# Keys of the second batch turned by a DMA transpose in place of TensorE transposes and ScalarE copies

## The chip, the cores and the metric

The kernel runs on one core of one Trainium2 chip. The time is the device time of one execution in microseconds (us), as the median of several executions. All runs told of here are in the fast state, with one core at work. A ratio is always the mean time of one kernel's fast runs over the mean time of the fast runs of the kernel before, of the same rounds on the same chip, so it is not quite the ratio of the medians that are quoted beside it. Intervals are 95% intervals.

## The reference

Sparse attention, then a gated feed-forward layer. There are 4 batches of 8 heads, 768 positions and 64 columns per head. Each query sees the keys less than 16 positions away, and 24 summaries of the keys (the maximum of each block of 32 keys, with the mean of the values of that block). The result, as 3072 tokens of 512 columns, goes through `x + sigmoid(x @ w_res) * ((gelu(x @ w_gate) * (x @ w_val)) @ w_out)`.

```python
k_sum = k.reshape(B, H, nb, block, D).max(axis=3)       # block maxima of the keys
v_sum = v.reshape(B, H, nb, block, D).mean(axis=3)      # block means of the values
scores_l = scale * np.matmul(q, k.transpose(0, 1, 3, 2))         # masked to |i - j| < 16
scores_s = scale * np.einsum('bhsd,bhnd->bhsn', q, k_sum) + np.log(block)
# softmax over both, times [v, v_sum], then the feed-forward layer
```

## The kernel before

The work is cut into 8 units of 384 tokens, two per batch. A unit has a gate/value stage of 12 column steps (g and vv matmuls, Gelu on ScalarE, a product on VectorE), and then an output stage, which also holds the scores and the attention of the next unit. During the two units of a batch, the keys, values and queries of the next batch are loaded and brought into place. The keys have to lie with the head's columns on the partitions, so they have to be turned. The batches from the third on do this with a DMA transpose; the second batch, which is loaded while the weights are still arriving, does it on TensorE.

```python
def load_k(b, t, i, n):            # one load of 768 KB (as bf16), 2 KB pieces of the source
    hs = slice(i * H // n, (i + 1) * H // n)
    nc.gpsimd.dma_start(out=t[:, hs]..., in_=k[b, hs].rearrange("h (p j) d -> p h (j d)", j=PJ))

def load_k_nat(b):                 # keys in order: twelve loads of 64 KB, 256-byte pieces
    k_nat = qk.tile([QT, NT, DM], BF16, tag="k_nat", name="k_nat")
    for t in range(NT):
        nc.gpsimd.dma_start(out=k_nat[:, t]..., in_=k[b, :, t * QT:(t + 1) * QT, :]...)
    return k_nat

def turn_k(b, k_nat):              # one DMA transpose of the whole batch, on SyncE's queue
    nc.sync.dma_start_transpose(out=kW[b % 2]...[:, :, 0:QT], in_=k_nat...)

def turn_pair(src, hp, pool, tag): # 16 transposes on TensorE for two heads
    ...
def k_place(b, hp, tp):
    nc.scalar.copy(kW[b % 2][:, :, hp, 0:QT]..., tp...)
    k_blocks(b, hp)                # block maxima, on VectorE: a reduce and a copy
    k_rims(b, slice(hp, hp + 1), nc.vector)   # keys of the neighbouring tiles

# ---- in the loop over units u and column steps fo (cut) ----
if half == 0 and nb == 1:          # first unit: loads of the second batch
    k_sb[nb] = k_tile()
    load_k(nb, k_sb[nb], 0, 1)
    v_loads(nb)                    # twelve loads of 64 KB
    load_q_nat(nb)                 # six loads of 128 KB
...
if half == 1 and nb < B:           # second unit of a batch
    if fo == 0:
        v_rims(nb, 0, HT)          # on SyncE's queue
        ...
    if fo == (4 if nb == 1 else 1):
        vsum_grp(nb, ps_t, "t")    # value sums: 12 matmuls over all twelve value tiles
        for i in range(4):
            vsum_bc(nb, 3 * i, 3 * i + 3, nc.gpsimd)   # copies of the value means
        turn_q(nb, 0)
        turn_q(nb, 1)
    if nb == 1:
        if fo < NP:
            k_step(nb, fo, ps_t, "t")      # turn_pair, then k_place
    elif 2 <= fo < 2 + NP:
        k_blocks(nb, fo - 2)
```

The softmax here doesn't subtract the row's maximum and nothing guards it: scores larger than these inputs give would overflow.

Of the kernel before, what the change touches and what calls it, by code (L numbers as in the profile page):

```python
# [15 lines left out]
def kernel(  # L16
# [11 lines left out]
    nc = tc.nc  # L28
# [16 lines left out]
    NP = H // 2  # L45
# [16 lines left out]
    ps_t = ctx.enter_context(tc.tile_pool(name="ps_t", bufs=1, space=bass.MemoryType.PSUM))  # L62
# [23 lines left out]
    def load_k(b, t, i, n):  # L86
        hs = slice(i * H // n, (i + 1) * H // n)
        nc.gpsimd.dma_start(out=t[:, hs].rearrange("p h j d -> p h (j d)"),
                            in_=k[b, hs].rearrange("h (p j) d -> p h (j d)", j=PJ))

    def k_tile():
        return qk.tile([PP, H, PJ, D], BF16, tag="k_sb", name="k_sb")
# [8 lines left out]
    def v_loads(b, lo=0, hi=NT):  # L101
        for t in range(lo, hi):
            nc.gpsimd.dma_start(out=vext[b % 2][0:QT, t, :, 0:D],  # L103
                                in_=v[b, :, t * QT:(t + 1) * QT, :].rearrange("h p d -> p h d"))

    def v_rims(b, lo, hi, eng=nc.sync):
        x = vext[b % 2]
        a, e = min(hi, NT - 1), max(lo, 1)
        eng.dma_start(out=x[QT:QT + WIN, lo:a], in_=x[0:WIN, lo + 1:a + 1])
        eng.dma_start(out=x[QT + WIN:BAND, e:hi], in_=x[QT - WIN:QT, e - 1:hi - 1])  # L110

    k_sb, q_sb = {}, {}

    def load_k_nat(b):
        k_nat = qk.tile([QT, NT, DM], BF16, tag="k_nat", name="k_nat")
        for t in range(NT):
            nc.gpsimd.dma_start(out=k_nat[:, t].rearrange("p (h d) -> p h d", d=D),  # L117
                                in_=k[b, :, t * QT:(t + 1) * QT, :].rearrange("h p d -> p h d"))
        return k_nat

    def load_q_nat(b):
        for c in range(NQ):
            nc.gpsimd.dma_start(out=q_nat[:, c].rearrange("p (h d) -> p h d", d=D),  # L123
                                in_=q[b, :, c * 128:(c + 1) * 128, :].rearrange("h p d -> p h d"))

    def turn_k(b, k_nat):
        nc.sync.dma_start_transpose(out=kW[b % 2].rearrange("d t g k -> d (t g) k")[:, :, 0:QT],
                                    in_=k_nat.rearrange("p t f -> p (t f)"))
# [6 lines left out]
    with tc.manual_schedule():  # L135
# [65 lines left out]
        def turn_pair(src, hp, pool, tag):  # L201
            tp = pool.tile([128, PJ, PP], BF16, tag=tag, name="tp")
            for j in range(PJ):
                for hh in range(2):
                    nc.tensor.transpose(tp[hh * 64:hh * 64 + 64, j, :], src[:, 2 * hp + hh, j, :],  # L205
                                        ident[0:PP, 0:PP])
            return tp

        def k_blocks(b, hp):
            kw = kW[b % 2][:, :, hp]  # L210
            ks = work.tile([128, NB], BF16, tag="ks", name="ks")
            nc.vector.tensor_reduce(  # L212
                out=ks.rearrange("d (t n) -> d t n", n=2),
                in_=kw[:, :, 0:QT].rearrange("d t (n w) -> d t n w", w=BLK),
                axis=mybir.AxisListType.X, op=ALU.max)
            nc.vector.tensor_copy(kw[:, :, BAND:BAND + NB], ks.unsqueeze(1).to_broadcast([128, NT, NB]))

        def k_rims(b, hps, eng):
            kw = kW[b % 2][:, :, hps]
            eng.tensor_copy(kw[:, 0:NT - 1, :, QT:QT + WIN], kw[:, 1:NT, :, 0:WIN])  # L220
            eng.tensor_copy(kw[:, 1:NT, :, QT + WIN:BAND], kw[:, 0:NT - 1, :, QT - WIN:QT])

        def k_step(b, hp, pool, tag):
            k_place(b, hp, turn_pair(k_sb[b], hp, pool, tag))

        def k_place(b, hp, tp):
            nc.scalar.copy(kW[b % 2][:, :, hp, 0:QT].rearrange("d t (p j) -> d t p j", j=PJ),
                           tp.rearrange("d j (t p) -> d t p j", t=NT))
            k_blocks(b, hp)
            k_rims(b, slice(hp, hp + 1), nc.vector)  # L230
# [367 lines left out]
        def pool_after(x):  # L598
            nc.gpsimd.tensor_copy(gate2[:], x)

        for u in range(NU):
            b, half = u // 2, u % 2
            nb = b + 1
            if half == 0 and nb == 1:
                k_sb[nb] = k_tile()
                load_k(nb, k_sb[nb], 0, 1)
                v_loads(nb)
                load_q_nat(nb)
            if u:
                gvT = upool.tile([128, FO, TU], BF16, tag="gvT", name="gvT")  # L610
            for fo in range(0 if u else 2, FO):
                if u > 1 and fo == 0:
                    fo_first(st, gvT)
                elif u and fo == FO - 2:
                    fo_last_two(st, gvT)
                elif u == 0 or fo < FO - 2:
                    fo_step(st, gvT, fo)
                if u == 0:
                    unit0_extras(fo)
                if u == 0 and fo >= 8:  # L620
                    q_step(1, fo - 8, ps_t, "t")
                if half == 0 and 1 < nb < B and fo == 0:
                    pool_after(st["xT"][0:1, KO - 1, 0:1])
                    k_nat = load_k_nat(nb)
                    v_loads(nb)
                if half == 0 and b and fo == 1:
                    v_rims(b, HT, NT)
                if half == 0 and 1 < nb < B and fo == 6:
                    turn_k(nb, k_nat)
                    k_rims(nb, slice(0, NP), nc.gpsimd)  # L630
                if half == 1 and nb < B:
                    if fo == 0:
                        v_rims(nb, 0, HT)
                        if nb > 1:
                            pool_after(st["xT"][0:1, KO - 1, 0:1])
                            load_q_nat(nb)
                    if fo == (4 if nb == 1 else 1):
                        vsum_grp(nb, ps_t, "t")
                        for i in range(4):
                            vsum_bc(nb, 3 * i, 3 * i + 3, nc.gpsimd)  # L640
                        turn_q(nb, 0)
                        turn_q(nb, 1)
                    if nb == 1:
                        if fo < NP:
                            k_step(nb, fo, ps_t, "t")
                    elif 2 <= fo < 2 + NP:
                        k_blocks(nb, fo - 2)
            if u == NU - 1:
                last_out(u, st, gvT)
            else:  # L650
                nst = new_unit()
                (mid_out if u else first_out)(u, st, gvT, nst)
                st = nst
# [30 lines left out]
```

## Time and profile before

| | before |
|---|---|
| median time | 260.93 us (260.77 to 261.4; three runs, a fourth, taken later, makes it 260.85) |
| span of the profiled execution | 260.5 us (this execution took 262.43 us, 1.5 more than the median) |
| TensorE (PE) busy | 251.3 us, 96% of the span |
| second unit, first gate matmul to the third unit's | 56.37 to 87.69 us: 31.3 us |

In all views PE is TensorE, PEld its loading of weights, DVE is VectorE, ACT ScalarE, POOL GpSimd and SP SyncE, which issues DMAs; a q behind the name marks work of the queue that the engine issues to. The granted clock is the share of TensorE's full clock that it was given. The profile's page of the kernel before has the busy time of each engine, and after it the span in 40 slices (each digit a busy share in tenths; PEclk the granted TensorE clock in tenths), and the chain of work that ended last:

```profile
PE 251.3 (96%) x2294; PEld 138.1 (53%) x2294; DVE 156.1 (60%) x344; ACT 126.3 (48%) x210; POOL 104.5 (40%) x142
...
PE   6999889999999999999999999999999999999993
...
PEclk9999999999999999999999999999999999999999
...
PE 82%; DMA 11%; POOL 3%; ACT 1%; issue 1%; DVE 1%; POOLq 0%
```

TensorE is the bound: it is 96% busy and 82% of the chain. What TensorE spends or saves in the second unit counts in full.

The timeline of the kernel before (start in us, length in us, engine, line, operation, output <- inputs, count, and in brackets the idle time before it and what ended it) shows one of the four key turns between two column steps, and the value sums:

```profile
57.02 0.81 PE L356 MATMUL vv<-xT,w_val 128*128 128x384 bf16 x4
...
57.77 0.53 PE L205 MATMUL tp<-ident,k_sb 96*64 96x96 bf16 x16
...
58.23 0.82 PE L356 MATMUL g<-xT,w_gate 128*128 128x384 bf16 x4
58.34 0.80 ACT L227 COPY kW<-tp 128x768 bf16<-128x768 bf16 x1 [0.35 <-PE tp L205]
...
65.23 0.83 PE L254 MATMUL vs<-vext,bgrp 64*32 64x512 bf16 x12
```

The chain of waits of the kernel before in the same stretch (start, length, what) is matmul after matmul. It tells what a turn costs: 0.46 us for the transposes and 0.11 us in the step behind them.

```profile
57.19 0.65 PE vv L356 x4
57.84 0.46 PE tp L205 x16
58.30 0.76 PE g L356 x4
59.05 0.65 PE vv L356 x4
```

The value sums (`vs`) at 65.23 us wait for nothing. For the loads, the view of the DMA issues (line, queue, size, median us from issue to landing) of one short window, in which two of the last value loads of the kernel before were issued:

```profile
vext<-in_v_dram POOLq DMA_DIRECT2D x2, 64.0 KB, 4.7
```

### The profile page before, as it was taken

How to read it: one execution, taken by the hardware profiler on the slowest of the kernel's cores; microseconds unless marked ns; L12 is line 12 of the kernel's file. 1: busy time of each engine (PE TensorE's matmuls, PEld its weight loads, DVE VectorE, ACT ScalarE, POOL GpSimd, SP SyncE). 2: the span in 40 equal slices, each digit the busy share in tenths (PEclk: the TensorE clock that was granted, in tenths of full speed). 3: DMA queues.
4: the chain of work that ended last, by engine and by line, in shares of the span. 5: the costliest groups of instructions: out<-in, count | busy, mean ns of one | idle time of the engine just before them, and what ended most of it. 6: DMA issues, size and time to landing. Idle time of an engine off the chain costs nothing.

```text
span 260.5 us, 5798 instructions
## 1 busy us (share of the span) xinstructions
PE 251.3 (96%) x2294; PEld 138.1 (53%) x2294; DVE 156.1 (60%) x344; ACT 126.3 (48%) x210; POOL 104.5 (40%) x142
## 2 busy tenths in 40 slices
PE   6999889999999999999999999999999999999993
PEld 2565444555555565545654565545654565556543
DVE  5945562579657644577858544778666544854424
ACT  6685337557373435623383437443493338253320
POOL 8896345266080689045250898064530000000000
PEclk9999999999999999999999999999999999999999
DMA  5999999999962899949912999959903500230002
GB/s 82 177 123 174 197 214 203 196 118 193 79 121 47 145 161 123 143 117 156 133 40 56 179 131 137 113 128 164 154 4 85 140 0 3 48 137 0 0 20 103
DMA packets 98155, 29.61 MB, mean 114 GB/s; under 512 B 83368, under 2 KB 94960, under 8 KB 98016
## 3 DMA queue, kind: packets, MB, share of 16 engines
q0 software_dynamic: 68400, 14.96, 69.0%
q1 hardware_dynamic: 29728, 14.29, 25.0%
q8 instruction: 18, 0.29, 0.5%
q14 instruction: 9, 0.07, 0.1%
HBM read 29.36 MB, written 6.29 MB: 137 GB/s over the span
## 4 chain that ended last, share of the span: by engine, by line
PE 82%; DMA 11%; POOL 3%; ACT 1%; issue 1%; DVE 1%; POOLq 0%
PE f L404 23%; PE g L356 22%; PE vv L356 22%; PE r L394 8%; DMA w_val<-in_moe_w_val_dram 5%; DMA w_gate<-in_moe_w_gate_dram 3%; DMA q_sb<-in_q_dram 3%; PE ao L316 3%; PE s L280 2%; POOL vext L103 1%; PE f L428 1%; PE vs L254 1%; PE tp L205 1%; POOL w_val L190 1%; POOL w_gate L189 1%
## 5 line engine op out<-in xcount | busy, mean ns | idle before, releaser
L362 DVE TENSOR_TENSOR gvT<-ge,vv 128x384 bf16<-128x384 f32 x96 | 52.9, 553 | 53.4 <-PE vv L356 48.5
L361 ACT ACTIVATE ge<-g 128x384 f32<-128x384 f32 x96 | 46.9, 490 | 73.5 <-DVE gvT L362 43.5
L356 PE MATMUL vv<-xT,w_val 128*128 128x384 bf16 x384 | 78.8, 326 | 1.3 <-DMA w_val<-in_moe_w_val_dram 1.3
L356 PE MATMUL g<-xT,w_gate 128*128 128x384 bf16 x384 | 78.8, 326 | 0.2
L404 PE MATMUL f<-w_out,gvT 128*128 128x512 bf16 x276 | 64.9, 380 | 0.0
L356 PEld LDWEIGHTS <-w_val 128*128 128x128 bf16 x384 | 37.3, 98 | 27.0 <-DMA w_val<-in_moe_w_val_dram 2.8
L356 PEld LDWEIGHTS <-w_gate 128*128 128x128 bf16 x384 | 36.7, 98 | 26.1 <-issue 1.6
L404 PEld LDWEIGHTS <-gvT 128*128 128x128 bf16 x276 | 25.7, 98 | 29.4 <-issue 0.3
L103 POOL DMA_DIRECT2D vext<-in_v_dram x48 | 32.6, 716 | 13.2 <-DMA w_out<-in_moe_w_out_dram 4.8
L397 ACT ACTIVATE th<-r 128x512 f32<-128x512 f32 x24 | 13.6, 604 | 28.4 <-PE r L394 28.4
L266 POOL COPY vext<-vsum 32x1536 bf16<-32x1536 bf16 x12 | 17.1, 1463 | 23.2 <-DMA vsum<-vpart 23.2
L410 DVE SCALAR_TENSOR_TENSOR th<-th,f 128x512 f32<-128x512 f32 (+1 forms) x25 | 16.5, 661 | 15.7 <-PE f L404 15.4
L302 DVE TENSOR_TENSOR P<-P,maskt 128x768 bf16<-128x768 bf16 x28 | 16.2, 581 | 12.6 <-ACT P L298 8.0
L394 PE MATMUL r<-w_res,xT 128*128 128x512 bf16 x96 | 23.2, 380 | 0.0
L336 DVE TENSOR_TENSOR xn<-ao,rz 128x384 bf16<-128x384 f32 x32 | 17.8, 557 | 1.1
L413 DVE SCALAR_TENSOR_TENSOR o<-th,xn 128x512 f32<-128x512 f32 (+1 forms) x25 | 17.3, 691 | 0.9
L298 ACT ACTIVATE P<-s,bias_t 128x768 bf16<-128x768 f32 x17 | 15.3, 901 | 4.7 <-PE s L280 4.5
L117 POOL DMA_DIRECT2D k_nat<-in_k_dram x24 | 16.4, 746 | 0.9 <-DMA k_nat<-in_k_dram 0.5
L123 POOL DMA_DIRECT2D q_nat<-in_q_dram x18 | 15.9, 918 | 0.8 <-issue 0.7
L295 ACT ACTIVATE P<-s,bias_t 128x384 bf16<-128x384 f32 x30 | 15.7, 578 | 0.3 <-PE s L280 0.3
L212 DVE TENSOR_REDUCE ks<-kW 128x24 bf16<-128x768 bf16 x16 | 15.1, 944 | 0.1
L394 PEld LDWEIGHTS <-xT 128*128 128x128 bf16 x96 | 8.8, 98 | 9.9
(85 smaller groups left out, 167.9 us busy)
## 6 DMA issues: line engine op xcount, KB each, us to landing
out_dram<-o SPq DMA_DIRECT2D x23, 256.0 KB, 2.3
vext<-in_v_dram POOLq DMA_DIRECT2D x48, 64.0 KB, 6.4
q_nat<-in_q_dram POOLq DMA_DIRECT2D x18, 128.0 KB, 7.7
w_gate<-in_moe_w_gate_dram POOLq DMA_DIRECT2D x6, 256.0 KB, 9.4
w_val<-in_moe_w_val_dram POOLq DMA_DIRECT2D x6, 256.0 KB, 10.8
w_out<-in_moe_w_out_dram POOLq DMA_DIRECT2D x3, 512.0 KB, 11.7
k_nat<-in_k_dram POOLq DMA_DIRECT2D x24, 64.0 KB, 4.8
vext<-vext SPq DMA_DIRECT2D x6, 144.0 KB, 6.1
```

The costliest lines, as they stand in the source:

```text
L103: nc.gpsimd.dma_start(out=vext[b % 2][0:QT, t, :, 0:D], in_=v[b, :, t * QT:(t + 1) * QT, :].rearrange("h p d -> p h d"))
L117: nc.gpsimd.dma_start(out=k_nat[:, t].rearrange("p (h d) -> p h d", d=D), in_=k[b, :, t * QT:(t + 1) * QT, :].rearrange("h p d -> p h d"))
L266: eng.tensor_copy(vext[b % 2][96:128, lo:hi, :, 0:D], src)
L302: nc.vector.tensor_mul(Pf, Pf, maskt.unsqueeze(1).to_broadcast([128, 2 * HT, QT]))
L336: nc.vector.tensor_mul(xn, ao[:, :, :, 0:D], rz.to_broadcast([128, NSUB, 2, D]))
L356: nc.tensor.matmul(ps[:, 0:TU], w[:, ko, fo * 128:(fo + 1) * 128], st["xT"][:, ko, :], start=(ko == 0), stop=(ko == KO - 1), skip_group_ch ...
L361: nc.scalar.activation(ge[:], g[:, 0:TU], AF.Gelu)
L362: nc.vector.tensor_mul(gvT[:, fo, :], ge[:], vv[:, 0:TU])
L394: nc.tensor.matmul(r[:], st["xT"][:, ko, ss], w_res[:, ko, :], start=(ko == 0), stop=(ko == KO - 1))
L404: nc.tensor.matmul(st["f", sub][:], gvT[:, fo, ss], w_out[:, fo, :], start=(fo == 0), stop=(fo == FO - 1), skip_group_check=True)
L410: nc.vector.scalar_tensor_tensor(th[:, cs], th[:, cs], 1.0, f[:, 0:n], ALU.add, ALU.mult)
L413: nc.vector.scalar_tensor_tensor(o.rearrange("p (k d) -> p k d", d=128), th[:, cs].rearrange("p (k d) -> p k d", d=128), 0.5, x, ALU.mult, ...
```

## The change

The four turns on TensorE, with their copies on ScalarE, are to go, and the second batch is to be treated like the later ones: its keys are loaded in order, turned by one DMA transpose at the start of the second unit, and the copies of the rims move to GpSimd. The block maxima come from the seventh column step on, to leave the transpose time.

```diff
             if half == 0 and nb == 1:
-                k_sb[nb] = k_tile()
-                load_k(nb, k_sb[nb], 0, 1)
+                k_nat = load_k_nat(nb)
                 v_loads(nb)
                 load_q_nat(nb)
@@
                 if half == 1 and nb < B:
                     if fo == 0:
+                        if nb == 1:
+                            turn_k(nb, k_nat)
+                            k_rims(nb, slice(0, NP), nc.gpsimd)
                         v_rims(nb, 0, HT)
@@
-                    if nb == 1:
-                        if fo < NP:
-                            k_step(nb, fo, ps_t, "t")
-                    elif 2 <= fo < 2 + NP:
-                        k_blocks(nb, fo - 2)
+                    kf = fo - (6 if nb == 1 else 2)
+                    if 0 <= kf < NP:
+                        k_blocks(nb, kf)
```

## The prediction

> **What bounds the kernel now.** TensorE. The page gives PE 251.3 us busy of a 260.5 us span (96%), at a granted clock of 0.9 or more in every slice; the chain of waits is 82% PE, and from 56 us on it is matmul after matmul without a gap. So there a microsecond of PE work removed is worth one, and a new PE wait costs one in full.
>
> **Removed.** In the second unit (56 to 75 us) the timeline shows four key turns on PE: each puts 16 small transposes between two 1.3 us column steps, and those steps then come 1.86 us apart (0.56 us each, four times, 2.2 us on the chain). Four ScalarE copies of 0.80 us and eight VectorE rim copies of 0.19 to 0.72 us go too, off the chain: worth nothing by themselves.
>
> **Added and moved.** One key load (0.79 us of GpSimd, issued at 37.7 us, landed at 54.0) becomes twelve of 64 KB. By the waits, GpSimd keeps eight loads in flight: each load waits for the eighth before it. So eight key loads go out in the existing gaps by 50.7 us (the last w_out lands near 50), the ninth at about 51, and from there 0.68 us each: keys until about 53.5, then all twelve value loads until about 61.5 (before: 57.6), then queries until about 67 (before: 62.9).
> On the DMA queue a whole-batch key transpose is issued after the three output stores, at about 59.2 us. In the next batch the same transpose holds SyncE 6.4 us and lands 11.3 us after its issue: about 70.5 us here. Beside it, value loads took 6.8 to 7.6 us to land against 3.0 to 3.4 just before it. So the last value loads, issued at 59 to 61 us, land near 67 to 68 us instead of 61.5. The Trainium skill ("DMA: Bandwidth & Descriptors", arbitration) says that a DMA engine round-robins between queue rows; the stretched landings agree.
>
> **On the critical path.** The value-sum matmuls stand after the fifth column step. Without the turns PE reaches them at about 63 us (before: 65.2), but they need all twelve value tiles. I expect a new PE wait of about 4 to 5 us ending near 67.7: the 2.2 us gain is used up and about 2.5 us lost. After that the block maxima on VectorE (0.95 + 0.23 us, four times, from the seventh step, about 71 us) find the keys just landed; PSUM buffers hide most of that. Queries land about 4 us later and are turned just before the scores need them (about 76 to 78 us). If the idle stretch gets longer than about 3.4 us, the clock may drop: "TensorE: Matmul & The Clock Gate" (Part 1) has such an idle window; this trace shows no drop. I count 0.4 us for it.
>
> **Prediction.** 263.5 us, 8 times in 10 between 260.2 and 266.8. Faster by over 2%: 0.01; within 2%: 0.86; slower by over 2%: 0.13.
>
> **Signs.** Right: value-sum matmuls wait on the value loads' DMA and start near 67 to 68 us; the scores of the third unit start near 78 us (before 75.2); span after that unchanged (about 185 us); key transpose lands near 70 us.
>
> **What would make it wrong.** Value loads landing by 63 us (then 259 to 260 us); the key transpose landing after 74 us, which blocks VectorE and then PE through PSUM; a clock drop (up to 3 us more); late queries.

## The result, and the profile after

The changed kernel takes 268.79 us (267.56 to 270.52, 4 runs) against 260.85 us (260.74 to 261.4): ratio 1.0305, interval 1.0246 to 1.0364. It is slower, by three times what was predicted, and the time lies outside the predicted range. The spans of the two profiles, 267.1 and 260.5 us, differ by less than the medians, because the profiled execution of before was 1.5 us slower than its median.

The page of the changed kernel:

```profile
PE 254.4 (95%) x2230; PEld 138.4 (52%) x2230; DVE 156.0 (58%) x336; ACT 123.5 (46%) x206; POOL 112.9 (42%) x155
...
PE   8999998993799999999999999999999999999994
...
PEclk9999999998589999999999999999999999999999
...
PE 79%; DMA 13%; POOL 4%; DVE 1%; issue 1%; ACT 0%
```

The share of TensorE in the chain fell to 79%, and one slice (the tenth, from 60 to 67 us) now shows TensorE 30% busy; in it and the two behind it the granted clock reads 8, 5 and 8 tenths.

The timeline of the changed kernel in the second unit, for the transpose, the value sums, the column step behind them, and GpSimd's copy of the key rims:

```profile
57.59 7.85 SPq L127 DMA_TRANSPOSE kW<-k_nat  x1
...
61.15 0.39 PE L254 MATMUL vs<-vext,bgrp 64*32 64x512 bf16 x2
...
61.74 0.37 PE L254 MATMUL vs<-vext,bgrp 64*32 64x512 bf16 x1 [0.21 <-DMA vext<-in_v_dram]
...
66.07 0.61 PE L254 MATMUL vs<-vext,bgrp 64*32 64x512 bf16 x4 [3.95 <-DMA vext<-in_v_dram]
...
68.04 1.27 PE L254 MATMUL vs<-vext,bgrp 64*32 64x512 bf16 x5 [1.36 <-DMA vext<-in_v_dram]
...
69.24 1.46 PE L356 MATMUL g<-xT,w_gate 128*128 128x384 bf16 x4
...
72.43 0.77 POOL L220 COPY kW<-kW 128x704 bf16<-128x704 bf16 x1 [5.20 <-DMA kW<-k_nat]
```

TensorE gets to the value sums at 61.15 us and stands before them, in pieces, until the last value tile has landed at 68.7 us. The chain of waits of the changed kernel says it in four lines: the last value load, issued at 59.73 us, is on its way for 8.96 us, and the next matmuls take 1.28 us in place of 0.65.

```profile
52.26 7.47 POOL vext L103 x11
...
59.73 8.96 DMA vext<-in_v_dram
...
68.73 0.58 PE vs L254
...
70.70 1.28 PE vv L356 x4
```

The DMA issues of the changed kernel in a window that holds one value load:

```profile
vext<-in_v_dram POOLq DMA_DIRECT2D x1, 64.0 KB, 9.0
```

A table of slices of two microseconds of the changed kernel (slice; its length and then the busy time of PE, PEld, DVE, ACT and POOL with counts; then the granted clock, the DMA share and GB/s):

```profile
62.00:64.00 2.00, 0.12 (x1) 0.00 (x0) 0.00 (x0) 0.00 (x0) 1.93 (x3) 1.00 1.41 151
64.00:66.00 2.00, 0.00 (x0) 0.00 (x0) 0.00 (x0) 0.00 (x0) 0.52 (x1) 0.65 1.51 183
66.00:68.00 2.00, 0.61 (x4) 0.11 (x4) 0.00 (x0) 0.00 (x0) 1.23 (x2) 0.50 1.81 146
...
70.00:72.00 2.00, 2.00 (x8) 0.91 (x7) 0.04 (x1) 0.49 (x1) 0.00 (x0) 0.50 2.20 150
...
74.00:76.00 2.00, 2.00 (x11) 1.14 (x10) 1.35 (x2) 0.49 (x1) 0.00 (x0) 0.79 1.79 138
```

TensorE is idle from 62.1 to 66.1 us, the clock falls to half, and it stays there until 74.8 us, more than five microseconds after TensorE has work again.

To compare without the weight loads at the start, whose length differs by up to 2.1 us between profiles (the second unit starts between 54.2 and 56.4 us in all the profiles told of here), I use **the stretch**: from the first gate matmul of the second unit to the first of the third, read from the timelines. It is 31.32 us before and 39.71 us after. Cut at the value sums and at the third unit's scores, the difference adds up:

| piece of the stretch (us) | before | after | difference |
|---|---|---|---|
| first gate matmul to value sums (the four turns are in it) | 8.86 | 6.60 | -2.26 |
| value sums to the next gate matmul | 0.76 | 8.09 | +7.33 |
| from there to the third unit's first scores (seven column steps) | 9.21 | 12.09 | +2.88 |
| from there to the third unit's first gate matmul | 12.49 | 12.93 | +0.44 |
| sum | 31.32 | 39.71 | +8.39 |

Behind the stretch nothing differs: from the third unit's first gate matmul to the end it is 172.8 us in both (from its first scores, which still lie in the stretch, 185.3 us before and 185.8 after).

So the intended gain is there, 2.26 us. It is buried under a wait for the values and a slow clock behind that wait.

### The profile page after: what moved, and what is told of

Read it like the earlier page. It is cut to its first block, busy times and chain, and to the rows that moved or that the text cites. A ratio compares the mean times of both kernels' runs of the same rounds, so it can differ in the third digit from the quotient of the medians.

```text
span 267.1 us, 5676 instructions
## 1 busy us (share of the span) xinstructions
PE 254.4 (95%) x2230; PEld 138.4 (52%) x2230; DVE 156.0 (58%) x336; ACT 123.5 (46%) x206; POOL 112.9 (42%) x155
## 4 chain that ended last, share of the span: by engine, by line
PE 79%; DMA 13%; POOL 4%; DVE 1%; issue 1%; ACT 0%
PE f L404 20%; PE g L356 20%; PE vv L356 19%; PE r L394 7%; DMA w_out<-in_moe_w_out_dram 5%; DMA q_sb<-in_q_dram 4%; PE wp L436 3%; DMA vext<-in_v_dram 3%; POOL vext L103 3%; PE s L280 2%; PE ao L316 2%; POOL k_nat L117 1%; PE vs L246 1%; PE f L428 1%; PE vs L254 1%
## 5 line engine op out<-in xcount | busy, mean ns | idle before, releaser
L356 PE MATMUL g<-xT,w_gate 128*128 128x384 bf16 x384 | 80.5, 331 | 0.2
L356 PE MATMUL vv<-xT,w_val 128*128 128x384 bf16 x384 | 80.1, 330 | 0.0
L356 PEld LDWEIGHTS <-w_gate 128*128 128x128 bf16 x384 | 37.5, 99 | 28.1 <-issue 4.0
L356 PEld LDWEIGHTS <-w_val 128*128 128x128 bf16 x384 | 37.9, 99 | 25.8 <-issue 1.6
L117 POOL DMA_DIRECT2D k_nat<-in_k_dram x36 | 24.5, 722 | 9.4 <-DMA w_out<-in_moe_w_out_dram 4.9
L302 DVE TENSOR_TENSOR P<-P,maskt 128x768 bf16<-128x768 bf16 x28 | 15.5, 558 | 11.6 <-ACT P L298 6.9
L394 PEld LDWEIGHTS <-xT 128*128 128x128 bf16 x96 | 8.9, 98 | 10.2 <-issue 0.2
```

Of the source, the lines that this page charges most:

```text
L117: nc.gpsimd.dma_start(out=k_nat[:, t].rearrange("p (h d) -> p h d", d=D), in_=k[b, :, t * QT:(t + 1) * QT, :].rearrange("h p d -> p h d"))
L356: nc.tensor.matmul(ps[:, 0:TU], w[:, ko, fo * 128:(fo + 1) * 128], st["xT"][:, ko, :], start=(ko == 0), stop=(ko == KO - 1), skip_group_ch ...
L394: nc.tensor.matmul(r[:], st["xT"][:, ko, ss], w_res[:, ko, :], start=(ko == 0), stop=(ko == KO - 1))
```

## The experiments

The theory is that the values are late because the transpose shares the DMA engines with them, that their lateness stops TensorE, and that the stop lowers the clock. The rivals are that the twelve loads alone do it, that a transpose is dear whatever stands behind it, and that the slow steps have another cause than the clock. "Value wait" in the table is the time from the first value-sum matmul to the end of the last, less the 0.83 us that they take without a wait.

| run | kernel | median us | ratio (interval) | stretch us | value wait us | half clock in the stretch us |
|---|---|---|---|---|---|---|
| (profile of before) | before | 260.85 | 1 | 31.3 | 0 | 0 |
| (profile of after) | after | 268.79 | 1.0305 (1.0246 to 1.0364) | 39.7 | 7.3 | 10.2 |
| c_after | after, again | 268.96 | 1.0299 (1.0244 to 1.0354) | 39.9 | 7.9 | 10.2 |
| e1_loads_only | before + twelve loads | 262.48 | 1.0043 (1.0005 to 1.0081) | 33.2 | 0 | 0 |
| e2_turn_only | before + unused transpose | 264.56 | 1.0131 (1.0091 to 1.0171) | 35.4 | 0 | 3.4 |
| e3_filler | after + filler matmuls | 268.72 | 1.0281 (1.024 to 1.0322) | 38.1 | filled | 0 |
| e4_vsum_late | after, value sums later | 274.99 | 1.0537 (1.048 to 1.0595) | 45.1 | 0.6 | 13.7 |
| e5_half_turn | after, half transposed | 267.25 | 1.0227 (1.0176 to 1.0278) | 38.4 | 4.8 | 6.8 |
| e6_fewer_ahead | after, eight key loads, late queries | 267.49 | 1.025 (1.0218 to 1.0282) | 36.1 | 1.9 | 3.4 |
| e7_copies_held | e1 + copies held | 262.32 | 1.0041 (1.0007 to 1.0074) | 32.0 | 0.2 | 0 |
| e8_turn_first | after, transpose before stores | 268.5 | 1.0257 (1.0207 to 1.0306) | 38.1 | 6.5 | 6.8 |
| e9_turn_first_8 | e8 + eight key loads | 266.7 | 1.0198 (1.0154 to 1.0242) | 37.3 | 4.5 | 6.8 |
| e10_first_held | e9 + copies held | 264.9 | 1.014 (1.0109 to 1.0171) | 34.7 | 4.0 | 3.4 |
| e11_first_late_q | e9 + late queries | 266.05 | 1.0178 (1.0147 to 1.0209) | 36.1 | 4.9 | 3.4 |
| e12_copy_only | before + unused plain copy | 263.42 | 1.0084 (1.0052 to 1.0116) | 34.1 | 0 | 0 |
| e13_after_values | after, transpose behind the values | 276.23 | 1.0575 (1.0545 to 1.0605) | 46.8 | 1.9 | 13.7 |
| e14_wide_turns | e7, eight loads, wider turns | 262.28 | 1.003 (0.9993 to 1.0067) | 31.7 | 0 | 0 |

All results were correct. The groups e1 to e4, c_after to e7, e8 to e11 and e12 to e14 each ran on one chip, beside runs of the kernel before with medians of 261.4, 261.06, 261.25 and 260.93 us. The length of the half clock is from the trace's clock records.

### Loads and transpose apart

**e1_loads_only** takes the loads alone; TensorE turns from the new layout.

```diff
-                k_sb[nb] = k_tile()
-                load_k(nb, k_sb[nb], 0, 1)
+                k_nat = load_k_nat(nb)
@@
-                            k_step(nb, fo, ps_t, "t")
+                            k_step_nat(nb, fo, k_nat)   # 24 transposes of 64 columns, one copy,
+                                                        # block maxima and rims as in k_place
```

> The kernel before with the twelve key loads of 64 KB in place of the one, and the keys still turned on TensorE (24 transposes of 64 columns per head pair, about the same 0.5 us of PE work). Theory A (the value loads are late because the key transpose runs beside them; the twelve loads alone only issue later): the last value load is issued near 60 us and lands within about 5 us, near 64 to 65 us; the value sums on TensorE wait less than 1 us; no clock drop; ratio to before 0.997 to 1.006. Rival B (the twelve loads alone are enough): the value sums wait until about 68 us and the clock drops; ratio at least 1.02.

Ratio 1.0043, and in the timeline of e1_loads_only the value sums run without a wait:

```profile
52.79 8.20 POOL L103 DMA_DIRECT2D vext<-in_v_dram  x12
...
63.97 0.83 PE L265 MATMUL vs<-vext,bgrp 64*32 64x512 bf16 x12
```

The value loads are issued from 52.79 to 60.99 us, just as late as in the changed kernel (52.22 to 60.41), and they are there at 63.97. Rival B falls: the loads alone don't hold the value sums until 68 us. But the margin is small. The last value tile lands at 63.66 us, 9.03 us after the start of the second unit (54.63), and TensorE comes at 63.97 only because it still does the turns. Without them it would come 6.6 us after the start, as in the changed kernel, and wait some 2.4 us (an estimate from these two distances). So a quarter to a third of the value wait of 7.3 us would come with the twelve loads alone, and it would use up the gain of 2.26 us; e13 measures 1.9 us for it. The stretch is 1.9 us longer: 0.5 us before the value sums and 1.4 us behind the third unit's first scores; the second part comes up under e7.

**e2_turn_only** takes the transpose alone: the same amount is transposed at the same place, and never read.

```diff
                     if fo == 0:
+                        if nb == 1:
+                            scrap = qk.tile([128, NT * NP, QT], BF16, tag="k_nat", name="scrap")
+                            nc.sync.dma_start_transpose(out=scrap[:],
+                                                        in_=w_gate[0:QT].rearrange("p k f -> p (k f)"))
                         v_rims(nb, 0, HT)
```

> The kernel before, with one unused DMA transpose of the same size (48 tiles of 64x128) issued at the place where the change issues the key transpose; its output is never read. Theory A: the value loads have been issued by 57.6 us, before the transpose starts, so they land by about 63 us and the value sums wait for nothing; query loads and turns come some 5 us later but still before the scores; ratio 0.998 to 1.008. Rival C (a big transpose on the queue is dear by itself, whatever stands behind it): ratio at least 1.02.

The values, issued before it, cause no wait, as expected. But the ratio is 1.0131, above what I expected, and below rival C's 1.02: the queries, which stand behind the transpose, now come too late, and the scores of the third unit wait for their turn. The waits of TensorE in e2_turn_only (who <- for what: us, times, longest):

```profile
PE s L280 <- DMA qT<-q_nat: 2.3, 1, 2.3
```

Two slices of the table of e2_turn_only (columns as before), the first with TensorE waiting, the second behind it at half clock:

```profile
74.00:76.00 2.00, 0.54 (x25) 0.48 (x25) 0.00 (x0) 0.15 (x1) 0.99 (x1) 1.00 0.76 164
...
78.00:80.00 2.00, 2.00 (x7) 0.59 (x4) 2.00 (x2) 0.78 (x2) 2.00 (x2) 0.50 0.00 0
```

So whichever load is still under way when the transpose starts pays. Loads alone cost 1.9 us of stretch, the transpose alone 4.1, both together 8.4, although 2.3 us of turns are gone with them. If the two costs simply added up, it would be 1.9 + 4.1 - 2.3 = 3.7 us. The rest comes with the loads still outstanding when the transpose starts, and with the longer half clock behind their wait (10.2 us in place of 3.4).

The trace's DMA records show why. Packets that ended in each slice of 2 us, on the software queue (128 bytes: loads of keys, values, queries) and on the hardware queue (256 bytes: the transpose; 2048 bytes: the output stores):

| slice us | after: software, transpose, stores | e1: software, stores | e2: software, transpose, stores |
|---|---|---|---|
| 58 to 60 | 1252, 0, 157 | 1158, 134 | 1085, 1, 127 |
| 60 to 62 | 1099, 360, 49 | 2060, 36 | 991, 519, 22 |
| 62 to 64 | 505, 927, 0 | 1996, 0 | 508, 998, 0 |
| 64 to 66 | 503, 1175, 0 | 610, 0 | 616, 880, 0 |
| 66 to 68 | 1066, 606, 0 | 2006, 0 | 1098, 668, 0 |
| 68 to 70 | 2374, 4, 0 | 2262, 0 | 2210, 6, 0 |

A value tile is 512 such packets. With no transpose the software queue moves 2000 packets in 2 us, four tiles; beside the transpose 500, one tile. (The 610 of e1 from 64 to 66 us stand beside the values' rim copies on the hardware queue, 23 packets of 7680 or 9216 bytes that the table leaves out.) The transpose has 3072 packets (786 KB in pieces of 256 bytes) and flows for 7.7 us, from 60.7 to 68.4 us, first held up by the output stores ahead of it. The Trainium skill, "DMA: Bandwidth & Descriptors" (Queues, rings and completion order), has each engine go round the queue rows that have work, one packet at a time, and counts some 9 to 17 descriptors to a packet; how the pieces of 128 and 256 bytes counted here are grouped, no view shows. The queues do share, but from that alone one can't tell that the shares come out as 927 to 505 and 1175 to 503. The same page's figure for a DMA transpose, 261 GB/s (Latency and other measured facts; measured there on one kernel, with a middle dimension that isn't contiguous), isn't met beside the loads: 786 KB in 7.7 us is 102 GB/s. It is nearly met where the loads are through. In the table of slices of e13_after_values (a run told of below; columns as before) the transpose has the engines to itself:

```profile
76.00:78.00 2.00, 0.00 (x0) 0.00 (x0) 0.00 (x0) 0.00 (x0) 0.00 (x0) 1.00 1.13 254
```

Nearly all of these 254 GB/s are 1977 packets of the transpose, with none of the software queue. So each of the two slows the other.

### The clock

**e3_filler** keeps TensorE busy through the wait.

```diff
                     if fo == (4 if nb == 1 else 1):
+                        if nb == 1:
+                            keep_warm(34)
                         vsum_grp(nb, ps_t, "t")
```

> The changed kernel with 34 filler matmuls of 512 columns (about 7.3 us) in front of the value sums of the second batch, so that TensorE isn't idle in the wait. Theory A's clock term (2.7 us of the loss is half clock after the idle wait, from 69.2 to 75.2 us in the profile): granted clock stays 1.00, the column steps after the wait take 1.3 us each instead of 2.56; the time falls by 2.0 to 3.2 us against the changed kernel: ratio to before 1.018 to 1.024. Rival: something other than the clock makes these steps slow, and the ratio stays at 1.03.

In the table of slices of e3_filler (columns as before) the clock stays at full speed:

```profile
66.00:68.00 2.00, 2.00 (x11) 0.93 (x10) 0.00 (x0) 0.00 (x0) 1.30 (x2) 1.00 1.46 169
...
70.00:72.00 2.00, 2.00 (x22) 0.99 (x15) 0.69 (x1) 0.49 (x1) 0.00 (x0) 1.00 2.57 188
```

From the step behind the value sums to the third unit's scores it takes 9.14 us, against 12.09 in the changed kernel and 9.21 before. The clock term is confirmed in the profile: 2.9 us. The time doesn't show it: the ratio is 1.0281 (1.024 to 1.0322), against 1.0305 and 1.0299 for the changed kernel in its two measurements, so the expected fall of 2.0 to 3.2 us was missed, and the small fall isn't clear of the noise. A part of it was lost again: from the scores to the third unit it takes 14.24 us in place of 12.93, because VectorE's first two mask multiplies took 3.50 us in place of 1.02. What that is, e7 shows. The filler lasts about as long as the wait that it covers: the value sums end 14.8 us after the start of the stretch in both kernels.

The Trainium skill, "TensorE: Matmul & The Clock Gate" (Part 1), says that the clock goes to half after about one idle window of 3.4 us, and back after a busy one. The changed kernel agrees with the first (4 us idle, then half); e2's stop of 2.3 us was enough as well, though, so a stop shorter than the window isn't safe. The half clock lasted 3.4, 6.8, 10.2 or 13.7 us in these runs. The clock records show why the place of a stop counts. In every profile each change of the clock falls on a grid of 3.41 us that starts at the trace's first clock record: in the changed kernel it drops after 17 steps, at 64.58 us, and is back after 3 more. By the matmul records (a few may be missing), TensorE was busy for 22% of the step before that drop, for 34% in e2 and at most 46% (e5) in all runs; the least busy step that no drop followed had 44% (e4). So a stop of 2.3 us can be enough if nearly all of it lies inside one step, as in e2.

### The second wait behind the first

**e4_vsum_late** takes the value wait off TensorE's way, by asking for the values later.

```diff
-                    if fo == (4 if nb == 1 else 1):
+                    if fo == (9 if nb == 1 else 1):
                         vsum_grp(nb, ps_t, "t")
```

> The changed kernel with the value sums of the second batch, the copies of them and the query turns moved from the fifth to the tenth column step, so that the wait for the value loads goes. Theory A with a second wait hidden behind the first (the turned keys land near 72 us, and the block maxima stand on VectorE after the seventh step, at about 64 us): VectorE waits for the turned keys, TensorE stops near 66 to 67 us for want of PSUM and goes on near 72 to 73; ratio 1.015 to 1.032. Rival D (the value loads alone are the cost): nothing waits until the tenth step; ratio 0.99 to 1.006.

The ratio is 1.0537: worse than I expected on either theory. The timeline of e4_vsum_late has the second wait, that of VectorE for the turned keys:

```profile
72.76 0.95 DVE L212 TENSOR_REDUCE ks<-kW 128x24 bf16<-128x768 bf16 x1 [8.05 <-DMA kW<-k_nat]
```

The chain of waits of e4_vsum_late has the length of the transpose:

```profile
57.83 14.91 DMA kW<-k_nat
```

The turned keys land 14.9 us after the issue of their transpose, where the next batch's took 11.3 in the profile of before. VectorE stands 8.1 us for them, and TensorE 7.6 us for VectorE's products, which free its PSUM (the memory that its matmuls write to); the value sums and the queries' turn, now later in the order, are late as well (the scores wait 2.7 us for the turned queries), and the clock drops twice. Taking away the wait that shows uncovers a wait as long. Rival D falls.

### Size and place of the transpose

**c_after** is the changed kernel again. It repeats its result.

> The changed kernel itself, unedited, as a control on the same chip as the three others. Measure used from here on beside the time: the stretch from the first gate matmul of the second unit to that of the third, which leaves out the weight loads at the start, whose length changes by up to 1.8 us from profile to profile. Stretches so far: before 31.3 us, changed 39.7, twelve loads alone 33.2, transpose alone 35.4, filler 38.1, value sums late 45.1. Expected here: stretch 38.9 to 40.5 us, ratio 1.025 to 1.036, half clock again after the wait.

**e5_half_turn** has six of twelve key tiles turned by DMA, six by TensorE.

```diff
+        n = HT if b == 1 else NT
-        nc.sync.dma_start_transpose(out=kW[b % 2].rearrange(...)[:, :, 0:QT],
-                                    in_=k_nat.rearrange("p t f -> p (t f)"))
+        nc.sync.dma_start_transpose(out=kW[b % 2][:, 0:n].rearrange(...)[:, :, 0:QT],
+                                    in_=k_nat[:, 0:n].rearrange("p t f -> p (t f)"))
@@
+                    if nb == 1 and fo < NP:
+                        k_half_pe(nb, fo, k_nat)       # the other six tiles on TensorE
+                        if fo == NP - 1:
+                            k_rims(nb, slice(0, NP), nc.gpsimd)
```

> The changed kernel with only the first six of the twelve key tiles turned by the DMA transpose, and the other six on TensorE (12 transposes of 64 columns per head pair and one copy of half the size). Theory A (cost grows with the bytes that the transpose puts beside the value loads): the last value tile lands 2 to 3 us earlier than in the changed kernel, the value sums wait 2 to 4 us in place of 7.3, the idle stretch is too short for the clock to drop or drops it only shortly, the keys land before 68 us; stretch 33.5 to 36 us, ratio 1.008 to 1.018. Rival F (a fixed cost of having any transpose on the queue): the wait stays over 6 us and the ratio at 1.025 or more.

A miss. The keys did land by about 68 us, but the value wait shrank only to 4.8 us and the clock still dropped, for 6.8 us. The half transpose flows until about 66 us and the last value tile lands at 68.5, hardly earlier than with the whole one. So the wait doesn't shrink in step with the bytes: the tiles still outstanding pile up behind the transpose, and come free together when it ends.

**e6_fewer_ahead** has less in the queue.

```diff
-        for t in range(NT):
-            nc.gpsimd.dma_start(out=k_nat[:, t]..., in_=k[b, :, t * QT:(t + 1) * QT, :]...)
+        if b == 1:
+            for h in range(H):
+                nc.gpsimd.dma_start(out=k_nat[:, :, h * D:(h + 1) * D],
+                                    in_=k[b, h].rearrange("(t p) d -> p t d", p=QT))
+            return k_nat
@@
-                load_q_nat(nb)
+                load_q_nat(nb, 0, NSUB)            # the second half after the copies of the means,
+                                                   # turned in the next unit
```

> The changed kernel with less in the queue beside and ahead of what is needed: the keys of the second batch in eight loads (one per head) in place of twelve, and the second half of the queries loaded only after the value sums have been copied and turned in the next unit. Theory A: GpSimd issues the last value load near 57.5 us, about when the transpose starts, in place of 59.9; the values land by 64 us and the value sums wait at most 2.5 us with no clock drop; the keys land near 70 us, so VectorE waits 4 to 6 us for them behind the seventh step and TensorE 2 to 4 us; stretch 31.5 to 35 us, ratio 1.000 to 1.014. Rival G (order and number of loads don't matter, the transpose delays them anyway): ratio 1.025 or more.

The value part went as expected: 1.9 us of wait, no drop there. The key part was worse: the keys landed 13.8 us after issue, at 72.9, VectorE waited 4.2 us for them, TensorE 3.7 us, and the clock dropped behind that. Ratio 1.025. Fewer loads ahead bring the values through, and the wait moves to the keys.

**e8_turn_first**, **e9_turn_first_8**, **e10_first_held** and **e11_first_late_q** issue the transpose ahead of the output stores, in the first unit's output stage.

```diff
             ffn_step(st, gvT, 0, 8, FO)
+            turn_k(1, k_nat)
             end_step(u, st, 0)
@@
                         if nb == 1:
-                            turn_k(nb, k_nat)
                             k_rims(nb, slice(0, NP), nc.gpsimd)
# e9, e10, e11: also eight key loads, as in e6;  e10: also copies held, as in e7;
# e11: also the second half of the queries late, as in e6
```

> The changed kernel with the key transpose issued ahead of the first unit's three output stores on the same queue, in place of behind them. The DMA records of the runs so far show the transpose's 256-byte packets only from about 61 to 68 us (issued at 57.6 to 58.3), after the last 2048-byte packets of the stores, and while they flow the software queue, which carries the values, moves about 215 packets per us in place of 1000. Theory A': if the transpose flows from 55 to about 61 us instead, the values come free 6 us earlier: the last lands near 63 to 65 us, the value sums wait 1 to 3.5 us with no clock drop, the keys land by 66 us and VectorE waits for them less than 1.5 us; stretch (second unit's first gate matmul to the third unit's) 30.5 to 34.5 us, ratio 0.995 to 1.012. Rival (the values are starved for as long whenever the transpose flows, because they are issued at a fixed pace behind it): last value at 66 us or later, ratio 1.016 or more.

> As the run before, and the keys of the second batch in eight loads (one per head) in place of twelve, so that keys and values are issued about 2.5 us earlier. Theory A': the transpose flows from about 53 to 59 us, the last value lands by 62.5 us, the value sums wait at most 1 us; what is left is the gain of 2.2 us from the removed turns less collisions of VectorE with GpSimd's copies; stretch 29 to 32 us, ratio 0.988 to 1.004. Rival: ratio above 1.012.

> As the second run of this call (transpose first, eight key loads), and the last two of the four copies of the value means held behind the third unit's first two mask multiplies. Expected 0 to 1.5 us less in the stretch than that run (28.8 to 31.5 us), ratio 0.986 to 1.002; if the copies don't meet the multiplies there, no difference.

> As the second run of this call (transpose first, eight key loads), and the second half of the queries loaded only after the copies of the value means. Theory A': with the queries' second half gone from the queue, nothing that is needed moves, since values and keys come ahead of the queries in it; the first half of the queries lands a little earlier; ratio within 0.004 of the second run. If the late queries had been holding up the transpose or the copies, it is faster by more than that.

The keys now come in time in all four: no key wait is left. But e8 and e9 miss, and the rival was right. The transpose, issued at 55.5 us in e8, flows from about 57 to 64 us; in the slice from 58 to 60 us the software queue moves 134 packets. The value loads, issued at 0.7 us each until 61 us, wait for its end all the same, and e8's last value tile lands at about 69 us. Not all of this is the transpose's doing: eleven tiles are there by 67.0 us, and the last comes at 68.9, while the output stores, now behind the transpose, move 292 packets of 2048 bytes in the slice from 66 to 68 us and the software queue 442. With eight key loads (e9) the values are issued earlier and land by 66.7 us, which leaves 4.5 us of wait. e10 misses too (ratio 1.014, at most 1.002 expected; stretch 34.7 us, at most 31.5 expected). It takes 2.6 us off e9's stretch, but not where it was meant to: the first two mask multiplies take 1.36 us in e9 and 1.35 in e10. Its half clock is 3.4 us shorter, and in e9 two copies of the block maxima took 1.40 and 1.47 us beside GpSimd's copies (0.23 without); how much is due to each I can't tell. e11 is within 0.004 of e9 as expected. Ahead of the stores or behind them, the transpose takes 7 to 8 us in which the loads hardly move, and both kinds of data are needed within the same 10 us.

**e13_after_values** has the transpose wait until the values are there.

```diff
                         if nb == 1:
+                            v_rims(nb, 0, NT)          # on the same queue, needs all value tiles
                             turn_k(nb, k_nat)
-                            k_rims(nb, slice(0, NP), nc.gpsimd)
-                        v_rims(nb, 0, HT)
+                        else:
+                            v_rims(nb, 0, HT)
@@
+                        if nb == 1:
+                            k_rims(nb, slice(0, NP), nc.gpsimd)   # behind the copies of the means
                         turn_q(nb, 0)
@@
-                    kf = fo - (6 if nb == 1 else 2)
+                    kf = fo - (8 if nb == 1 else 2)
```

> The changed kernel with the key transpose held on its queue until all value tiles have landed (it stands behind all their rim copies), the rim copies of the keys behind the copies of the value means, and the block maxima from the ninth column step on. If the transpose alone starves the values: the last value lands by 65 us as with the loads alone, the value sums wait at most 1.5 us more than there (they come at about 61 to 62 us, so 2 to 3.5 us in all), no clock drop there; and the wait comes back at the keys, which land near 73 us: VectorE waits for them from about 67 us and TensorE stops for 4 to 6 us; ratio 1.012 to 1.032. Rival (the values are late because of the loads): values still land at 68 us.

Its first half is what the theory says. With all the loads of the changed kernel, and the transpose starting later, the timeline of e13_after_values has the value sums nearly on time. The 1.9 us that are left come from the later loads, without any transpose beside them:

```profile
61.99 0.39 PE L254 MATMUL vs<-vext,bgrp 64*32 64x512 bf16 x3
...
63.28 0.82 PE L254 MATMUL vs<-vext,bgrp 64*32 64x512 bf16 x8 [0.90 <-DMA vext<-in_v_dram]
...
64.34 0.37 PE L254 MATMUL vs<-vext,bgrp 64*32 64x512 bf16 x1 [0.23 <-DMA vext<-in_v_dram]
...
87.26 0.23 PE L280 MATMUL s<-qT,kW 64*128 64x64 bf16 x2 [13.34 <-POOL kW L220]
```

The second half is far worse than I expected, ratio 1.0575. The rim copies of the values, now in one piece, stand ahead of the transpose on its queue with packets of 16,896 bytes, and its own packets come only from about 73 us on. The third unit's scores then wait 13.3 us for GpSimd's key rims, which I had put behind the copies of the value means. The end of this run is thus partly of my own making, and only its value wait is used as evidence.

### Is it the transpose as such?

**e12_copy_only** puts a plain copy of 786 KB, also in 256-byte pieces, where e2 has the transpose.

```diff
-                            nc.sync.dma_start_transpose(out=scrap[:],
-                                                        in_=w_gate[0:QT].rearrange("p k f -> p (k f)"))
+                            nc.sync.dma_start(out=scrap.rearrange("p (a c) k -> p a (c k)", c=2),
+                                in_=w_gate.rearrange("p k (a c) -> p (k a) c", c=256)[:, :, 0:128])
```

> The kernel before with one unused plain copy in place of the unused transpose of the earlier run: same queue, same place, same 786 KB from SBUF to SBUF, in pieces of 256 bytes as well (3072 of them). Theory S (the starving of the software queue comes from the transpose as such): the copy's packets are through in 3 to 5 us, the software queue keeps more than 400 packets per us beside them, the third unit's scores don't wait for the query turn; stretch 31 to 33 us, ratio 0.998 to 1.006. Rival B2 (any 786 KB in 256-byte pieces on that queue starves it alike): the copy's packets take 7 us or more, the software queue falls to some 250 packets per us, and the ratio is that of the unused transpose, 1.010 to 1.017.

Between the two. Its packets flow for 8 us or more, and the software queue falls to 706, 785 and 971 packets per 2 us (508, 616 and 1098 beside the transpose). The third unit's scores wait 1.25 us for the turned queries, against 2.3, and the clock doesn't drop; ratio 1.0084 against 1.0131 (1.0052 to 1.0116 and 1.0091 to 1.0171, which overlap). So most of it comes with a plain copy of the same bytes on the other queue too, and a transpose seems to take somewhat more. The size of the pieces wasn't varied in a run of its own, but large ones starve the loads as well: beside the values' rim copies of e13 (9 packets of 16,896 bytes in the slice from 70 to 72 us) the software queue moved 363 packets, with three query loads still outstanding. How much more a transpose takes, and why the hardware queue gets the larger share, these runs don't settle.

### The copies that meet the mask

**e7_copies_held** is e1 with two of the four copies of the value means held back.

```diff
-                        for i in range(4):
+                        for i in range(2 if nb == 1 else 4):
                             vsum_bc(nb, 3 * i, 3 * i + 3, nc.gpsimd)
@@
             s_step(n, 1, nst, TO2)
+            if u == 1:
+                pool_after(nst["P", 1][0:1, 0, 0, 0:1])
+                vsum_bc(1, 6, 9, nc.gpsimd)
+                vsum_bc(1, 9, 12, nc.gpsimd)
```

> The kernel with twelve loads alone, and in addition the last two of the four GpSimd copies of the value means held back until the third unit's first two mask multiplies are done (they are not needed before the fourth unit). Theory H (the 3.2 us that VectorE's two mask multiplies took there in place of 1.1 is a collision with the GpSimd copies): the two multiplies take 0.55 to 0.6 us each, the stretch falls from 33.2 to 30.8 to 32 us; ratio to before 0.993 to 1.001. Rival: the multiplies are slow for another reason; stretch near 33.2, ratio 1.004.

The timeline of e1_loads_only around the third unit's first two mask multiplies (VectorE, `P<-P,maskt`):

```profile
72.22 6.02 POOL L277 COPY vext<-vsum 32x1536 bf16<-32x1536 bf16 x4 [5.97 <-DMA vsum<-vpart]
...
75.48 3.17 DVE L313 TENSOR_TENSOR P<-P,maskt 128x768 bf16<-128x768 bf16 x2 [0.81 <-ACT P L309]
```

The timeline of e7_copies_held, the same two multiplies and the next two:

```profile
76.45 0.56 DVE L313 TENSOR_TENSOR P<-P,maskt 128x768 bf16<-128x768 bf16 x1 [0.81 <-ACT P L309]
...
77.39 0.56 DVE L313 TENSOR_TENSOR P<-P,maskt 128x768 bf16<-128x768 bf16 x1 [0.39 <-ACT P L306]
...
79.89 2.11 DVE L313 TENSOR_TENSOR P<-P,maskt 128x768 bf16<-128x768 bf16 x2
```

The two multiplies take 0.56 us each when no GpSimd copy runs, and the stretch falls from 33.2 to 32.0 us, the edge of what I expected. The collision is shown. The Trainium skill, "SBUF — State Buffer" (Who interferes with whom), says that a VectorE instruction with two inputs in SBUF contends with a GpSimd instruction that reads SBUF. That fits: the multiply reads two tiles, and GpSimd's copy reads one. In the time the gain isn't seen (1.0041 against 1.0043, in different groups), and a part of it only moves: the next two multiplies, at 79.89, now meet the held copies. In the kernel before the first two took 1.70 us, so it pays a little of this too; in e3 it was 3.50.

**e14_wide_turns** was to keep the gain without the transpose.

```diff
-            for t in range(NT):
-                for hh in range(2):
-                    h = 2 * hp + hh
-                    nc.tensor.transpose(tp[hh * 64:hh * 64 + 64, t, :], kn[:, t, h * D:(h + 1) * D],
-                                        ident[0:QT, 0:QT])
+            for t in range(NT):
+                nc.tensor.transpose(tp[:, t, :], kn[:, t, hp * 128:(hp + 1) * 128], ident[0:QT, 0:QT])
# and eight key loads, as in e6
```

> A candidate: no DMA transpose. The keys of the second batch come in eight loads in key order and are turned on TensorE in 12 transposes of 128 columns per head pair (both heads at once, which this order allows) in place of 16 of 64 columns by 96; copies of the value means held as in the run e7_copies_held. Expected: 0.15 to 0.25 us less per head pair on TensorE than there, values land in time; stretch 30.5 to 31.8 us; ratio to before 0.996 to 1.003. It beats the kernel before only if the values no longer wait and the four turns get below 0.4 us each.

Ratio 1.003, interval 0.9993 to 1.0067: not faster. A turn of 12 wide transposes still takes 0.52 us in the timeline, where the 24 narrow ones of e7 took 0.56 and the 16 of the kernel before 0.53. The expected saving of 0.15 to 0.25 us was missed: the count of instructions wasn't what a turn costs. No version here beats the kernel before.

## Why the prediction was right or wrong

- **What bounds the kernel: right.** TensorE, with its wait paid in full; behind the stretch both kernels take the same (172.8 us).
- **The gain: right in size.** Predicted 2.2 us, measured 2.26 before the value sums. It was never to be had in full, though: the twelve loads alone bring the values later than TensorE without its turns (e1, e13: 1.9 to 2.4 us of wait).
- **The mechanism of the loss: right.** The value sums wait for value loads that the transpose delays. e1 (no transpose, same loads: last value 9.0 us after the start of the unit, against 14.1) and e13 (same loads, transpose later: 1.9 us of wait, against 7.3) show it.
- **The size of the value wait: wrong.** The step that failed is "I expect a new PE wait of about 4 to 5 us ending near 67.7". Measured: 7.3 us, ending at 68.7 (7.9 in the second profile). Counted from the start of the second unit, TensorE's arrival was right: 6.6 us predicted (63 less 56.4) and 6.60 measured; only the unit itself started 1.8 us earlier than in the profile of before. What was wrong is the landing of the last value: 11.3 us predicted (67.7 less 56.4), 14.1 measured. The load was issued some 0.6 us later in the unit than I had thought, and took 9.0 us from issue to landing, not the 6.8 to 7.6 that I had read from a later batch, where neither output stores stood ahead of the transpose nor query loads behind the values. Which of the two matters was not tried alone in this kernel; e11, with half of the query loads gone, had its last value no earlier than e9 (67.3 and 66.7 us).
- **The clock: wrong, and the larger mistake of judgement.** "I count 0.4 us for it." Measured: 2.88 us in the profile, and e3 gives the same from the other side (9.14 us for those steps with the clock kept, 12.09 without). A predicted wait of 4 to 5 us and a window of 3.4 us, both in the same text, should have made the drop the expected case.
- **The sum.** Predicted: -2.2 + 4.7 + 0.4, or +2.9 us (the stated 263.5 us is 2.65 over the median of before, 260.85). Measured in the stretch: -2.26 + 7.33 + 2.88 + 0.44 = +8.39 us. In the medians it is +7.9.
- **The key transpose near 70 us: wrong by its length.** GpSimd could copy the key rims only at 72.4 us, 14.8 us after the issue; I had taken 11.3. The last data packet ended at 68.4 us, and the completion came 4.0 us behind it; in e13, with no loads beside the transpose, 0.5 us behind it (77.9 and 78.4 us). Why, no run shows. In the changed kernel this hides behind the value wait; e4 and e6 bring it out.
- **Named, but not counted:** the late queries. In the changed kernel they hide behind the value wait; e2 brings them out (2.3 us). **Missed altogether:** the collision of mask multiplies with GpSimd's copies (e1, e3). Both decide how much of a repaired wait comes back.

What stays open: why the hardware queue gets the larger share of the engines beside the loads, how much the transpose, as against a plain copy of the same bytes, adds to that, and why its completion came so long after its data.

## What to carry to other kernels

Moving work from a busy engine to the DMA queues is only free if nothing that is needed soon is still under way there: look at what the queues carry in the same microseconds and when each piece is due, and take the time of the moved transfer from a place with the same company. When you predict a wait, ask at once whether it is long enough to lower the clock behind it, and which wait stands next in line; a repaired wait gives back only the distance to the next one. And read arrival times from several profiles, or as distances inside a stretch, not from one profile's absolute times.

## What the Trainium skill lacked or had wrong

- "DMA: Bandwidth & Descriptors" (Latency and other measured facts) gives a DMA transpose 261 GB/s and no figure beside other traffic. e13 comes near it with nothing else on the queues (254 GB/s). Beside loads on another queue the changed kernel's 786 KB flowed for 7.7 us (102 GB/s), and landed 13.8 to 14.9 us after issue (e6, e4, and the changed kernel). The page doesn't say what a transpose leaves to the other queues: about 500 packets of 128 bytes per 2 us in place of 2000.
- The same page's round-robin over queue rows (Queues, rings and completion order) gives no shares in bytes or time. Measured beside 128-byte loads: 927 to 1175 transpose packets against about 505, and 1218 and 890 packets of a plain copy against 706 and 785.
- "TensorE: Matmul & The Clock Gate" (Part 1) gives an idle window of about 3.4 us before the clock drops, but not how much work a window may hold and still count as idle. Here drops followed steps of 3.41 us in which TensorE was busy for 34% (e2, with a stop of 2.3 us) and in one case 46% (e5), while one of 44% (e4) was followed by none. In the changed kernel half clock lasted 10.2 us, more than five of them with TensorE at work again.
- "SBUF — State Buffer" (Who interferes with whom) gives the contention of VectorE and GpSimd as two ratios, 6.8 and 1.5 times slower, without the instructions behind them. Here two mask multiplies of 0.56 us each took 3.17 to 3.50 us together (e1, e3) under GpSimd copies of 1.47 us, and a copy then took up to 1.79 us.
